# Clamp and low-half subtraction of the weight conversions on GpSimd instead of VectorE, in a pooled attention with two feed-forward products

## The chip, the cores and the metric

The kernel runs on one core of a Trainium2 chip. The metric is the device time of one execution in microseconds (us), the median of several runs. TensorE (PE) multiplies, VectorE (DVE) and ScalarE (ACT) work element by element, GpSimd (POOL) does so too and issues a part of the DMAs, and SyncE (SP) issues the rest.

## The reference

Everything is float32; `moe_w1` and so on are drawn in double precision and are handed over as 64-bit numbers.

```python
# attention: 8 batches, 8 heads, 576 positions, head width 64; k and v are averaged over 8 positions
k_p = k.reshape(B, H, Sp, 8, D).mean(axis=3);  v_p = v.reshape(B, H, Sp, 8, D).mean(axis=3)
attn = softmax(q @ k_p.T / sqrt(D));           x = attn @ v_p          # then 4608 x 512
# first feed-forward
h = ((x @ w1) * (x @ w2)) @ w3                 # 512 -> 1024 -> 1024
x = h @ w_out                                  # 1024 -> 512
# second feed-forward
g = max(x @ w_in, 0) + log1p(exp(-abs(x @ w_in)))    # 512 -> 2048
out = g @ w_out2                               # 2048 -> 512
```

## The kernel before

The kernel first multiplies w3 by w_out (W, 1024 x 512), since nothing stands between the two products: 64 full float32 products `Wp` (L509, in W_mm). Then, block by block of 512 tokens, it computes a = x w1, b = x w2, g = a b and x2 = g W (`ab`, `x2_mm`), while the attention of later tokens runs between these products. Last comes the second feed-forward. Products in the main loops are made of three passes over a high and a low half of each operand (`mm3`, L122 to L124; `split`, L117 and L118).

The weights lie in memory as 64-bit words. w_out, w3, w1 and w2 come in 20 jobs of two tiles of 128 x 512 each: 12 for w_out and w3 (four and eight), 8 for the groups of w1 and w2 (`w12_0` to `w12_7`). A job is: two loads by SP into a ring of four raw places (L130), so that two jobs are in flight; `magnitudes`, the absolute value of the upper word on ACT (L137); then `convert_steps` on DVE: clamp (L146), shift (L148), sign (L151), bits of the lower word (L156). The groups of w1 and w2 are then split: the high half on ACT (L160), the low half by a subtraction on DVE (L163). While one job is between L151 and L156, `ahead` begins the next one: its L137 is issued there. When a job is over, its two raw places are loaded again.

The names in the rows: `wgh_512_...` and `wgl_512_...` are the converted tiles of w_out and w3, `w_0h` and `w_0l` are the two halves of a group of w1 or w2, `area_f` holds raw words and staging, `area_r` the halves that TensorE reads, `ks`, `kT` and `vb` are the averaged keys and values, `sc`, `pr`, `pT` and `pv` the steps of the attention.

Each engine works through its instructions in the order in which the program issues them; the order is written out by hand: a table of slots for the attention (`sched`, run by `att_slot`) and a list of background steps (`bg`) that advances the jobs by one or two steps per slot. GpSimd's own queue before holds the loads of k, v and q (L305, L312, L315) and the copies of the averaged keys (L328).

Of the kernel before, what the change touches and what calls it, by code (L numbers as in the profile page):

```python
# [8 lines left out]
F32 = mybir.dt.float32  # L9
# [3 lines left out]
ALU = mybir.AluOpType  # L13
# [21 lines left out]
HI_MIN = 3.4332275390625e-05 * HI_SCALE  # L35
HI_MAX = 122879.9921875 * HI_SCALE
# [12 lines left out]
def pooled_attention_two_ffn(ctx: ExitStack, tc: tile.TileContext, qT_d, kT_d, v_d, w12_d, w3T_d, wo_d, wi_d, wo2_d, out):  # L49
# [3 lines left out]
    nc = tc.nc  # L53
# [55 lines left out]
    def t2k(name, dt=F32):  # L109
        return t2k_ring[0]([P, 512], dt)  # L110
# [22 lines left out]
    def magnitudes(raws, dsts, name):  # L133
        both = range(len(raws))
        y = dsts or [t2k(f"y_{name}_{i}") for i in both]
        for i in both:
            nc.scalar.activation(y[i], raws[i][:, :, 1].bitcast(F32), AF.Abs, scale=HI_SCALE)  # L137
        return y

    def convert_steps(raws, dsts, y, ahead):  # L140


        both = range(len(raws))
        yi = [t.bitcast(I32) for t in y]
        for i in both:
            nc.vector.tensor_scalar(y[i], y[i], HI_MIN, HI_MAX, op0=ALU.max, op1=ALU.min)  # L146
        for i in both:
            nc.vector.tensor_scalar(yi[i], yi[i], 3, None, op0=ALU.logical_shift_left)  # L148
        yield
        for i in both:  # L150
            nc.vector.scalar_tensor_tensor(yi[i], raws[i][:, :, 1], -0x80000000, yi[i], op0=ALU.bitwise_and, op1=ALU.bitwise_or)  # L151
        yield
        ahead()
        yield
        for i in both:
            nc.vector.scalar_tensor_tensor(yi[i], raws[i][:, :, 0], 29, yi[i], op0=ALU.logical_shift_right, op1=ALU.bitwise_or)  # L156
        yield
        if isinstance(dsts[0], tuple):
            for i in both:
                nc.scalar.activation(dsts[i][0], y[i], AF.Copy)  # L160
            yield
            for i in both:
                nc.vector.tensor_sub(dsts[i][1], y[i], dsts[i][0].bitcast(F32))  # L163

# [12 lines left out]
    def begin_job(k):  # L179
        if len(loaded) > k:  # L180
            name, raws, dst, split_ = loaded[k]
            if name not in begun:
                dsts = None if split_ else dst()
                begun[name] = dsts, magnitudes(raws, dsts, name)

    def next_job():
        load_ahead()
        begin_job(0)
        name, raws, dst, _ = loaded[0]
        dsts, y = begun.pop(name)  # L190
        yield from convert_steps(raws, dsts or dst(), y, lambda: begin_job(1))
        loaded.pop(0)
        converted.add(name)
        load_ahead()
# [699 lines left out]
```

## Time and profile before

| | us |
|---|---|
| median of 3 runs | 1573.36 (1571.50 to 1576.69) |
| span of the profiled execution, first to last instruction | 1572.0 |
| TensorE busy | 1525.3 |
| VectorE busy | 1002.8 |
| ScalarE busy | 769.4 |
| GpSimd busy | 138.6 |

The page gives the span of the profiled execution and no other time for it; the span lies 1.4 us under the median and inside the three runs. Busy shares are means over stages with different limits: the conversions of w_out, w3, w1 and w2 lie in the first 170 us alone. In a timeline row, the first two numbers are start and length in us; "x2" means that two instructions of one form are merged, and what stands in brackets is the engine's idle time ahead of them and what ended it.

### The profile page before, as it was taken

What the parts mean: (1) busy time and instruction counts of PE and PEld (TensorE: products, weight loads), DVE (VectorE), ACT (ScalarE), POOL (GpSimd) and SP (SyncE); (2) the same over time, 40 slices, a digit from 0 to 9 for tenths busy, and PEclk for the clock granted to TensorE, in tenths of its full rate; (3) what the DMA queues carried; (4) which work ended last, traced back from release to release, by engine and by line L of the source; (5) the groups of instructions that cost most, each with busy time, mean ns of one, the idle gap of its engine ahead of it and who ended that gap; (6) DMA issues with size and microseconds to landing.
All of it is one profiled execution on the core that took longest, in us unless ns stands there. A gap on an engine that the chain in (4) does not pass through costs nothing.

```text
span 1572.0 us, 20121 instructions
## 1 busy us (share of the span) xinstructions
PE 1525.3 (97%) x7712; PEld 1283.2 (82%) x7712; DVE 1002.8 (64%) x1514; ACT 769.4 (49%) x1611; POOL 138.6 (9%) x266
## 2 busy tenths in 40 slices
PE   4889999999999999999999999999999999999998
PEld 2448788888888888777889889898988898989897
DVE  7886666556565654222346777677777677678665
ACT  3445444444444443332245566566556556556554
POOL 3200101010100100000110000000000000000000
PEclk9999999999999999999999999999999999999999
DMA  8553244435453532003445336335336335434431
GB/s 287 195 183 122 59 163 153 148 124 182 138 187 129 192 109 72 1 27 134 134 155 179 121 114 202 114 123 193 124 112 204 110 128 167 152 111 130 149 105 40
DMA packets 70943, 215.21 MB, mean 137 GB/s; under 512 B 6848, under 2 KB 26304, under 8 KB 63680
## 3 DMA queue, kind: packets, MB, share of 16 engines
q0 software_dynamic: 24352, 124.79, 24.8%
q1 hardware_dynamic: 46496, 89.14, 16.5%
q8 instruction: 61, 1.00, 0.3%
q14 instruction: 34, 0.28, 0.1%
HBM read 171.97 MB, written 41.94 MB: 136 GB/s over the span
## 4 chain that ended last, share of the span: by engine, by line
PE 91%; DVE 4%; ACT 2%; DMA 2%; issue 1%; POOL 0%; SPq 0%; DVEq 0%; ACTq 0%; POOLq 0%
PE o L766 8%; PE o L765 8%; PE ab L122 8%; PE o L764 8%; PE ab L124 8%; PE ab L123 8%; PE X L123 4%; PE X L124 4%; PE X L122 4%; PE x2p L122 4%; PE x2p L124 4%; PE x2p L123 4%; PE Z L123 3%; PE Z L122 3%; PE Z L124 3%; PE pv L397 2%
## 5 line engine op out<-in xcount | busy, mean ns | idle before, releaser
L117 ACT ACTIVATE area_r<-area_f 128x768 fp32r<-128x768 f32 (+1 forms) x168 | 126.7, 754 | 224.9 <-DVE area_f L563 183.9
L766 PE MATMUL o<-w2h,area_r 128*128 128x512 f32 x576 | 228.2, 396 | 0.3 <-DVE area_r L118 0.3
L765 PE MATMUL o<-w2l,area_r 128*128 128x512 f32 x576 | 227.2, 394 | 0.0
L764 PE MATMUL o<-w2h,area_r 128*128 128x512 f32 x576 | 224.0, 389 | 0.0
L118 DVE TENSOR_TENSOR area_r<-area_f,area_r 128x768 fp32r<-128x768 f32 (+1 forms) x168 | 141.7, 844 | 116.6 <-ACT area_r L117 116.4
L733 ACT ACTIVATE area_f<-area_f 128x768 f32<-128x768 f32 x96 | 81.3, 847 | 124.9 <-DVE area_f L825 123.4
L737 DVE TENSOR_SCALAR area_f<-area_f 128x768 f32<-128x768 f32 x96 | 53.8, 560 | 120.2 <-ACT area_f L734 120.2
L123 PE MATMUL X<-area_r,wf 128*128 128x384 f32 x384 | 129.2, 336 | 0.0
L124 PE MATMUL X<-area_r,wf 128*128 128x384 f32 x384 | 128.9, 336 | 0.0
L122 PE MATMUL X<-area_r,wf 128*128 128x384 f32 x384 | 128.8, 335 | 0.0
L766 PEld LDWEIGHTS o<-w2h,area_r 128*128 128x128 f32 x576 | 108.0, 187 | 23.6 <-DVE area_r L118 0.7
L362 ACT ACTIVATE pr<-sc,mx 128x72 f32<-128x72 f32 x288 | 87.7, 331 | 80.5 <-DVE mx L360 80.5
L563 DVE TENSOR_TENSOR area_f<-area_f,ab 128x512 f32<-128x512 f32 x72 | 49.4, 686 | 115.1 <-PE ab L124 108.4
L764 PEld LDWEIGHTS o<-w2h,area_r 128*128 128x128 f32 x576 | 108.2, 188 | 16.0 <-ACT area_r L117 0.3
L765 PEld LDWEIGHTS o<-w2l,area_r 128*128 128x128 f32 x576 | 108.0, 187 | 15.9
L634 POOL DMA_DIRECT2D wf<-wis x96 | 51.9, 541 | 774.5 <-PE X L124 665.5
L122 PE MATMUL x2p<-area_r 128*128 128x512 f32 x288 | 115.8, 402 | 0.0
L124 PE MATMUL x2p<-area_r 128*128 128x512 f32 x288 | 112.6, 391 | 0.0
L123 PE MATMUL x2p<-area_r 128*128 128x512 f32 x288 | 112.4, 390 | 0.0
L123 PE MATMUL Z<-area_r,wf 128*128 128x384 f32 x288 | 96.8, 336 | 0.0
L743 DVE TENSOR_TENSOR area_f<-area_f 128x768 f32<-128x768 f32 x96 | 92.0, 958 | 6.7 <-ACT area_f L740 0.5
L122 PE MATMUL Z<-area_r,wf 128*128 128x384 f32 x288 | 96.2, 334 | 0.0
(167 smaller groups left out, 3334.5 us busy)
## 6 DMA issues: line engine op xcount, KB each, us to landing
wf<-wis POOLq DMA_DIRECT2D x48, 1024.0 KB, 5.2
wf<-wis POOLq DMA_DIRECT2D x48, 768.0 KB, 4.5
area_f<-in_wo_dram SPq DMA_DIRECT2D x24, 512.0 KB, 4.3
wis<-area_f SPq DMA_DIRECT2D x40, 256.0 KB, 2.6
kv<-in_kT_dram POOLq DMA_DIRECT2D x32, 288.0 KB, 3.9
q<-in_qT_dram POOLq DMA_DIRECT2D x18, 512.0 KB, 5.0
kv<-in_v_dram POOLq DMA_DIRECT2D x32, 288.0 KB, 4.5
x2d<-area_f SPq DMA_DIRECT2D x36, 256.0 KB, 4.0
```

The source lines that it names most:

```text
L117: nc.scalar.activation(hi, src, AF.Copy)
L118: nc.vector.tensor_sub(lo, src, hi.bitcast(F32))
L122: nc.tensor.matmul(ps, whi, xhi, start=first, stop=False, skip_group_check=resumed)
L123: nc.tensor.matmul(ps, whi, xlo, start=False, stop=False, skip_group_check=resumed)
L124: nc.tensor.matmul(ps, wlo, xhi, start=False, stop=last, skip_group_check=resumed)
L362: nc.scalar.activation(pr[:, h, :], sc[h // 4][:, h % 4, :], AF.Exp, bias=mx[:, h:h + 1], scale=SCALE, accum_out=sm[:, h:h + 1])
L733: nc.scalar.activation(e, c, AF.Abs)
L737: nc.vector.tensor_scalar(u, e, 1.0, None, op0=ALU.add)
L743: nc.vector.tensor_add(c, c, u)
L764: nc.tensor.matmul(oacc[s][i], hl[:, 0, ts], wh, start=first, stop=False)
L765: nc.tensor.matmul(oacc[s][i], hl[:, 0, ts], wl, start=False, stop=False)
L766: nc.tensor.matmul(oacc[s][i], hl[:, 1, ts], wh, start=False, stop=last)
```

## The change

The clamp (L146 before) is taken out of `convert_steps` and issued in `magnitudes` on GpSimd, right behind the absolute value of each tile. The subtraction of the low half (L163 before) is issued on GpSimd at the same point of the program. All of the 20 jobs are concerned by the first edit (40 clamps), the 8 jobs of w1 and w2 by the second (16 subtractions). `convert_1024`, the conversion of the second feed-forward's weights, is left as it is.

```diff
 def magnitudes(raws, dsts, name):
     for i in both:
         nc.scalar.activation(y[i], raws[i][:, :, 1].bitcast(F32), AF.Abs, scale=HI_SCALE)
+        nc.gpsimd.tensor_scalar(y[i], y[i], HI_MIN, HI_MAX, op0=ALU.max, op1=ALU.min)
     return y
 def convert_steps(raws, dsts, y, ahead):
...
-    for i in both:
-        nc.vector.tensor_scalar(y[i], y[i], HI_MIN, HI_MAX, op0=ALU.max, op1=ALU.min)
     for i in both:
         nc.vector.tensor_scalar(yi[i], yi[i], 3, None, op0=ALU.logical_shift_left)
...
         for i in both:
-            nc.vector.tensor_sub(dsts[i][1], y[i], dsts[i][0].bitcast(F32))
+            nc.gpsimd.tensor_sub(dsts[i][1], y[i], dsts[i][0].bitcast(F32))
```

From here on the changed kernel has one line less: its L138 is the clamp, its L162 the subtraction, and every other line of the places below has a number that is smaller by one.

GpSimd's queue around the second batch's averaged keys, before (`ks_1` is the second of four pieces; `kv_1_0` is a load of v):

```order
L328 COPY kT_109<-ks_0_449 64x72 x2
L312 DMA kv_0_3_453<-in_kT_dram 128x576
L328 COPY kT_109<-ks_1_472 64x72 x2
L315 DMA kv_1_0_476<-in_v_dram 72x1024
L328 COPY kT_109<-ks_2_513 64x72 x2
L315 DMA kv_1_1_517<-in_v_dram 72x1024
L305 DMA q_537<-in_qT_dram 128x1024
```

The same place in the changed kernel (`wgl_512_320`, `wgh_512_480` and `wgl_512_481` are the jobs wo6, w3_6 and w3_7):

```order
L138 TENSOR_SCALAR wgl_512_320<-wgl_512_320 128x512 x2
L327 COPY kT_109<-ks_0_449 64x72 x2
L311 DMA kv_0_3_453<-in_kT_dram 128x576
L327 COPY kT_109<-ks_1_472 64x72 x2
L314 DMA kv_1_0_476<-in_v_dram 72x1024
L138 TENSOR_SCALAR wgh_512_480<-wgh_512_480 128x512 x2
L327 COPY kT_109<-ks_2_513 64x72 x2
L314 DMA kv_1_1_517<-in_v_dram 72x1024
L138 TENSOR_SCALAR wgl_512_481<-wgl_512_481 128x512 x2
L304 DMA q_539<-in_qT_dram 128x1024
```

The clamps of a job now stand in GpSimd's queue behind copies and loads of the attention, and loads of k, v and q behind clamps.

VectorE's queue over the same stretch, before:

```order
L146 TENSOR_SCALAR wgl_512_320<-wgl_512_320 128x512 x2
L148 TENSOR_SCALAR wgl_512_320<-wgl_512_320 128x512 x2
L325 TENSOR_REDUCE ks_0_449<-kv_0_0_194 128x72
L151 SCALAR_TENSOR_TENSOR wgl_512_320<-area_f,wgl_512_320 128x512 x2
L325 TENSOR_REDUCE ks_1_472<-kv_0_1_211 128x72
L156 SCALAR_TENSOR_TENSOR wgl_512_320<-area_f,wgl_512_320 128x512 x2
L146 TENSOR_SCALAR wgh_512_480<-wgh_512_480 128x512 x2
L148 TENSOR_SCALAR wgh_512_480<-wgh_512_480 128x512 x2
L151 SCALAR_TENSOR_TENSOR wgh_512_480<-area_f,wgh_512_480 128x512 x2
L118 TENSOR_TENSOR area_r<-pv_486,area_r 128x4x128
```

And in the changed kernel:

```order
L147 TENSOR_SCALAR wgl_512_320<-wgl_512_320 128x512 x2
L324 TENSOR_REDUCE ks_0_449<-kv_0_0_196 128x72
L150 SCALAR_TENSOR_TENSOR wgl_512_320<-area_f,wgl_512_320 128x512 x2
L324 TENSOR_REDUCE ks_1_472<-kv_0_1_213 128x72
L155 SCALAR_TENSOR_TENSOR wgl_512_320<-area_f,wgl_512_320 128x512 x2
L147 TENSOR_SCALAR wgh_512_480<-wgh_512_480 128x512 x2
L150 SCALAR_TENSOR_TENSOR wgh_512_480<-area_f,wgh_512_480 128x512 x2
L118 TENSOR_TENSOR area_r<-pv_488,area_r 128x4x128
```

Two instructions per job are gone from VectorE, and the shift (L147) is now the first of a job there; it waits for GpSimd, where L146 waited for ScalarE. ScalarE's, TensorE's and SyncE's own orders stay as they were.

## Rows read from the trace of the kernel before

**Rows 1.** The page's first part: busy time, share of the span, instructions.

```profile
PE 1525.3 (97%) x7712; PEld 1283.2 (82%) x7712; DVE 1002.8 (64%) x1514; ACT 769.4 (49%) x1611; POOL 138.6 (9%) x266
```

**Rows 2.** Stretches: busy us (instructions) by engine, TensorE's granted clock, DMA share, GB/s.

```profile
0.00:110.00 110.00, 79.07 (x257) 39.88 (x257) 88.88 (x175) 45.65 (x122) 23.93 (x47) 0.91 0.71 235
110.00:175.00 65.00, 62.59 (x354) 50.74 (x353) 46.43 (x92) 31.60 (x98) 6.51 (x12) 1.00 0.31 100
```

**Rows 3.** Chain that ended last, in order of time: start, us, what.

```profile
12.14 6.45 DMA kv<-in_v_dram
...
20.96 0.67 DVE wgl L146 x2
...
34.43 4.44 DMA area_f<-in_w3T_dram
38.89 0.69 ACT wgl L137
39.60 0.43 DVE wgl L146
...
40.61 1.29 DVE wgl L151 x2
...
58.06 0.67 DVE wgl L146 x2
...
65.53 0.67 DVE wgl L146 x2
...
70.59 0.67 DVE wgh L146 x2
...
77.31 8.96 DMA area_f<-in_w_dram
...
87.48 1.98 PE pv L397 x16
89.45 20.77 PE Wp L509 x44
```

**Rows 4.** TensorE's waits from 0 to 110 us: us in total, times, longest.

```profile
PE pv L397 <- ACT pT L380: 4.0, 1, 4.0
```

**Rows 5.** The two moved lines by themselves: ns shortest/median/longest, first and last start.

```profile
L146 DVE TENSOR_SCALAR wgh<-wgh x12: 417/420/427, 5.0 to 70.8; 128x512 f32<-128x512 f32 x12
L163 DVE TENSOR_TENSOR w_0l<-area_f,w_0h x2: 679/680/681, 93.0 to 93.6; 128x512 fp32r<-128x512 f32 x2
```

**Rows 6.** GpSimd's timeline at the start, and its copies (L328) by themselves.

```profile
0.25 0.10 POOL L882 MEMSET const-float32-0.0<- 128x1 f32 x1 [0.25 <-issue]
...
0.74 0.20 POOL masks.py:197 MEMSET ident<- 128x128 f32 x1 [0.29 <-POOLq L882]
1.03 0.29 POOL masks.py:199 TENSOR_SCALAR_AFFINE_SELECT ident<-ident 128x128 f32<-128x128 f32 x1
...
L328 POOL COPY kT<-ks x64: 236/243/3591, 10.6 to 602.4; 64x72 f32<-64x72 f32 x64
```

**Rows 7.** Timelines of GpSimd, then of VectorE, from 69 to 74 us.

```profile
69.65 3.87 POOL L328 COPY kT<-ks 64x72 f32<-64x72 f32 x2
73.47 0.53 POOL L315 DMA_DIRECT2D kv<-in_v_dram  x1
...
69.31 1.28 DVE L156 SCALAR_TENSOR_TENSOR wgl<-area_f,wgl 128x512 int32<-128x512 int32 x2
70.51 0.76 DVE L146 TENSOR_SCALAR wgh<-wgh 128x512 f32<-128x512 f32 x2
71.18 0.76 DVE L148 TENSOR_SCALAR wgh<-wgh 128x512 int32<-128x512 int32 x2
71.86 1.28 DVE L151 SCALAR_TENSOR_TENSOR wgh<-area_f,wgh 128x512 int32<-128x512 int32 x2
73.06 0.69 DVE L118 TENSOR_TENSOR area_r<-pv,area_r 128x512 fp32r<-128x512 f32 x1
```

**Rows 8.** TensorE's waits from 100 to 200 us: us in total, times, longest.

```profile
PE pTp L379 <- DVE pr L370: 3.1, 3, 1.7
```

**Rows 9.** Timelines of ScalarE and TensorE: last group's high half, first use of its low half.

```profile
167.24 1.14 ACT L160 ACTIVATE w_7h<-area_f 128x512 fp32r<-128x512 f32 x2
...
173.41 0.39 PE L124 MATMUL ab<-area_r,w_7l 128*128 128x512 f32 x1
```

## The prediction

> **What bounds the kernel now.** I read the busy shares first: TensorE is busy for 97% of the span [rows 1]. Only stretches in which it waits can be moved by an edit on other engines, so the next view is the one by stretches. Up to 110 us TensorE works for 79 us, with the other 31 us lost at the start and between products, while VectorE is busy for 89 of the 110 and the DMA engines for 71%; from 110 to 175 us TensorE waits for 2.4 us in all [rows 2]. All 20 jobs that the change touches lie in these two stretches; what follows is the same work in the same order, and it starts earlier or later by what they gain or lose.
>
> So the third view is the chain of work that ended last, within the first 110 us [rows 3]. It runs through a load of v at 12 us, several conversions of w_out and w3 on VectorE, a load of raw words at 34 us, an absolute value and a clamp at 39 us, the second load of raw words at 77 us, and from 89.45 us through 44 products in a row. Two points of it matter. The load at 77.31 us can start only when VectorE has ended job w3_6, since it takes that job's raw places; it takes 8.96 us. And TensorE's wait of 4.0 us ahead of the pv products at 87.48 us is a wait for ScalarE's copy [rows 4], which stands in ScalarE's queue behind the absolute value that wants this load. Whatever makes w3_6 end later on VectorE therefore shifts 87.48 us, and everything behind it, by as much.
>
> **What is taken off VectorE.** A clamp lasts 0.42 us by itself and a low half 0.68 us [rows 5]; in a row two clamps take 0.67 us of VectorE's time [rows 3], and two low halves overlap in the same way, so I count 1.2 us for them, an estimate. That is 20 times 0.67 and 8 times 1.2, some 23 us of VectorE's 1003. It is no gain by itself: only the clamps on the chain count.
>
> **What one costs on GpSimd.** No such clamp or subtraction runs there before, so I bound it by GpSimd's own rows [rows 6]. A memset of one column takes 0.10 us and one of 128 columns 0.20 us, which is 0.0008 us a column over a fixed 0.10; the affine select reads and writes 128 columns in 0.29 us, 0.0015 a column; a copy of 72 columns takes 0.243 us, 0.0020 a column over the same 0.10. For 512 columns this gives 0.51, 0.86 and 1.12 us; the copy taken as a plain ratio of columns gives 1.73. I take c = 0.86 us for a clamp, since the affine select is the row that is most like it (all partitions, one input, one output, arithmetic in between), with 0.51 and 1.73 as the ends. A subtraction reads a second input: I add a memset's 0.0008 a column and take s = 1.3 us, between 0.86 and 3.46 (twice 1.73). The Trainium skill (GPSIMD Engine Reference, Engine selection) says that one-input work on GpSimd runs at about line rate and two-input work at about half of VectorE's speed. An estimate from that page, 512 columns at its 1.2 GHz, would be 0.43 us for the clamp; by it the sum below would be about 0.
>
> **Can they run beside VectorE?** This is the point on which the sum rests. Two copies on GpSimd that take 0.24 us each stood there for 3.87 us from 69.65 us. VectorE went through L156, L146, L148 and L151 in that time without a gap, and the copies ended when it came to L118, which reads PSUM and one operand of SBUF [rows 7]. So GpSimd doesn't get at SBUF while VectorE runs conversion steps back to back: neither between two of them nor beside them. A clamp on GpSimd runs when VectorE waits, reduces or reads PSUM; otherwise it runs when VectorE has come to the shift that needs it, and then both clamps of the job are paid in full.
>
> **Term by term, up to 110 us.**
> - T1, clamps that are ready in time. At three places of the chain (20.96, 27.03 and 58.06 us; the first and the last in [rows 3]) VectorE ahead of the clamp reduces, waits or reads PSUM, so the clamps are over and 0.67 us goes away: 3 times -0.67 = -2.0 us.
> - T2, the job clamped at 65.53 us (wo6). Its absolute values are written while VectorE normalizes and runs L156. Both clamps then follow one another: 2c - 0.67 = +1.05 (ends +0.35 and +2.79). The same happens at 34.3 us, off the chain: the load at 34.43 us covers it [rows 3].
> - T3, the job at 39.60 us, whose words arrive last of all. From the end of the absolute value (39.58) to the sign step (40.61) it is 1.03 us now [rows 3]; a clamp of c and a shift of 0.42 in its place make c - 0.61 = +0.25 (ends -0.10 and +1.12).
> - T4, the job clamped at 70.59 us (w3_6). Its clamps stand in GpSimd's queue behind the two copies of `ks_1` and the load of `kv_1_0`. The copies can't start before VectorE has ended L156 of the job ahead, as they couldn't before [rows 7]. VectorE's shift thus waits for two copies (0.49), the issue of a DMA (0.53) and two clamps, against 0.67 now: 0.49 + 0.53 + 2c - 0.67 = +2.07 (ends +1.37 and +3.81). This is the largest term, a wait in the place of the work removed; behind that shift on VectorE stand L118 and the maxima, and TensorE's scores wait for L118.
> - T5, the load of v at 12.14 us on the chain [rows 3]. It is now issued behind both clamps of the second job; 0 to 2c later, and I take half, c = +0.86.
> - T6, w3_7's second clamp, which may hold SBUF when VectorE wants it for w3_6's last step: 0 to c, and I take a third, +0.3.
>
> Sum: -2.0 + 1.05 + 0.25 + 2.07 + 0.86 + 0.3 = +2.5 us.
>
> **From 110 to 175 us.** TensorE waits for VectorE's normalization three times, 3.1 us in all [rows 8]. What is ahead of each is the product of a and b, ScalarE's copy and exp; no clamp or low half is in that chain, so none of it is won. A clamp of the next job can hold SBUF when the normalization is due: 0 to c, taken at half, +0.4. The low halves have time. The tightest is the last group's: its high half ends at 168.38 us and TensorE wants the low one at 173.41 [rows 9], 5.0 us for two subtractions of 2s = 2.6 us.
>
> Together +2.9 us, or 6.83c - 2.93 as a function of c. Against the profiled execution, 1572.0 + 2.9 = 1574.9 us; its span is 1.4 us under the median, so on the median's scale 1573.4 + 2.9 = **1576 us**. A measurement of this kernel can tell about 0.3% (4.7 us) from no change, so this forecast is "no change that can be told".
>
> **The rivals.**
> - Slower: GpSimd's clamp is dear. One mechanism, T2, T4 and T5 with a larger c. By the function above the shift reaches 4.7 us at c = 1.12 us, which is what the copy's rate gives; at c = 1.73 it is +8.9 us, 1582 us. For it: the copies are the only rows of GpSimd that read computed data and write it elsewhere, and rows 7 show how long it can be kept off SBUF. Against it: most of a copy's 0.24 us may be fixed cost.
> - Faster: GpSimd does run beside VectorE, and the copies of rows 7 waited for something else. Then the five pairs of clamps on the chain go at 0.67 us each, -3.35, and the load of 77.31 us, which begins earlier, may find the DMA engines freer; -3 to -6 us, 1567 to 1570 us. Against it stands every instant of [rows 7].
> - Fair turns: GpSimd waits for the instruction that runs on VectorE, not for the whole row of them. T4's copies and DMA would then be over when L156 ends and T4 falls by 0.49 + 0.53 = 1.0: +1.9 us, 1575 us. The Trainium skill (SBUF — State Buffer, SBUF: two separate sides) describes the pair of ports shared by VectorE and GpSimd as a lock that whoever starts first holds for one whole instruction, which would allow such turns; the 3.87 us in rows 7 span eight instructions and speak against it.
> - The edit does nothing: the load of 8.96 us at 77.31 us shrinks by what it starts later, and TensorE's wait of 4.0 us swallows the rest: 1573 us. I count it with the forecast, since it has no sign.
>
> **How the numbers follow.** Forecast (c between 0.51 and 1.12, or the case without effect): 0.55, no change that can be told. Fair turns: 0.10, the same. Dear clamp: 0.25, slower by over 0.3%. Side by side: 0.10, half of it within 0.3% and half faster. So faster 0.05, same 0.70, slower 0.25. The low end is the forecast with c = 0.51 and T5, T6 and the normalization at nothing: -2.0 + 0.35 - 0.10 + 1.37 = -0.4, that is 1573, less 2 us for the spread of the runs and the edge of the side-by-side case: 1571. The high end reaches to the dear clamp's 1582. What lies outside is the faster half of one rival and subtractions dearer still.
>
> **What would show it.** In the profile of the changed kernel: a clamp of 0.8 to 0.9 us where VectorE is idle, and stretched ones where it isn't (c); VectorE waiting for GpSimd at the shift of wo6, w3_3 and w3_6, with some 2 us at w3_6 (T2 to T4); no wait at the shifts of w3_1, wo2 and w3_5 (T1); the load of w12_0 starting near 80 us instead of 77.31 and TensorE's 44 products ending near 112.7 instead of 110.2; the stretch from 175 us on as long as now. The forecast is wrong if VectorE's conversion steps get longer while GpSimd works, if GpSimd's clamps start between two of them, or if TensorE comes to wait for a low half.

## The result, and the profile after

The changed kernel takes 1593.0 us in the median (1592.28 to 1594.9, 4 runs) against 1574.12 us before (1571.5 to 1576.69, 4 runs): a ratio of 1.012, with a 95% interval from 1.0104 to 1.0136. That is +18.9 us (16.4 to 21.4), where the prediction had +2.9 and a range that ended at 1582. The profiled execution has a span of 1591.6 us, 19.6 more than before.

The page's busy shares come first; they answer to [rows 1].

```profile
PE 1527.5 (96%) x7712; PEld 1284.1 (81%) x7712; DVE 997.8 (63%) x1458; ACT 770.5 (48%) x1611; POOL 242.9 (15%) x322
```

Fifty-six instructions have gone to GpSimd, and its busy time rose by 104 us. VectorE lost the same 56 but only 5.0 us of busy time. The prediction had counted some 23 us taken off VectorE. TensorE works 2.2 us longer, so nearly all of the loss is waiting.

The view by stretches (columns as in [rows 2]) says where; the third stretch is one within the second.

```profile
0.00:110.00 110.00, 68.01 (x233) 34.12 (x234) 74.04 (x126) 38.15 (x109) 80.79 (x76) 0.89 0.65 213
110.00:175.00 65.00, 58.42 (x282) 42.86 (x281) 45.06 (x65) 30.96 (x79) 46.05 (x28) 0.95 0.33 107
...
125.00:130.00 5.00, 5.00 (x13) 3.84 (x13) 5.00 (x9) 2.33 (x5) 2.04 (x2) 0.50 0.30 120
```

TensorE works 68.0 instead of 79.1 us up to 110 us, and 58.4 instead of 62.6 from there to 175. The loss is where the prediction looked for it.

The chain of work that ended last, in order of time, answers to [rows 3]. Before, the chain's only steps on GpSimd were copies of keys and the issue of a load, up to 12.1 us.

```profile
42.59 3.97 POOL wgl L138 x2
...
57.05 4.71 DMA area_f<-in_w3T_dram
62.53 4.58 POOL wgl L138 x2
...
71.90 4.26 POOL wgl L138 x2
...
81.10 3.81 POOL wgh L138 x2
...
89.03 4.27 POOL wgl L138 x2
...
109.19 4.40 POOL w_0l L162 x2
113.59 3.78 POOL area_f L138 x2
...
118.80 2.76 DVE area_f L150 x2
122.26 1.17 ACT w_2h L159 x2
```

A pair of clamps (L138) takes 3.8 to 4.6 us on the chain, where [rows 3] had 0.67 us for a pair on VectorE. The next view has groups of the two moved lines by themselves (ns shortest/median/longest, first and last start), as [rows 5] had them on VectorE.

```profile
L138 POOL TENSOR_SCALAR wgh<-wgh x12: 1904/1912/2368, 5.0 to 83.0; 128x512 f32<-128x512 f32 x12
L138 POOL TENSOR_SCALAR wgl<-wgl x12: 1904/2164/3251, 18.3 to 90.9; 128x512 f32<-128x512 f32 x12
L162 POOL TENSOR_TENSOR w_0l<-area_f,w_0h x2: 1261/2215/3169, 109.2 to 112.3; 128x512 fp32r<-128x512 f32 x2
L162 POOL TENSOR_TENSOR w_6l<-area_f,w_6h x2: 1287/1292/1297, 172.6 to 173.9; 128x512 fp32r<-128x512 f32 x2
```

The clamp takes 1.91 us where it is undisturbed, above the upper end that the prediction gave it (1.73), and up to 3.25 us. The subtraction takes the 1.3 us that it was taken at, but one of w_0l takes 3.17. Undisturbed, the instruction with one input is dearer than the one with two.

What VectorE waits for, until the end of w3_6's last step (us in total, times, longest): first the whole list after, to 91.6 us, then the two rows of the kernel before that answer to its first two, to 77.3 us.

```profile
DVE wgh L147 <- POOL wgh L138: 16.6, 8, 7.0
DVE wgl L147 <- POOL wgl L138: 5.0, 6, 1.1
DVE sm L367 <- ACT pr L361: 3.9, 3, 1.6
DVE vb L335 <- DMA kv<-in_v_dram: 2.9, 2, 2.3
DVE ks L324 <- POOL kT L327: 1.5, 1, 1.5
DVE mx L358 <- PE sc L347: 1.5, 2, 1.1
...
DVE wgh L146 <- ACT wgh L137: 7.0, 4, 5.0
DVE wgl L146 <- ACT wgl L137: 1.1, 2, 0.8
```

And the stretch up to that step's end by engine (columns as in [rows 2]), before and after, with e15 (below), in which nobody clamps, as the third.

```profile
0.00:77.24 77.24, 50.69 (x178) 26.63 (x179) 61.09 (x125) 29.84 (x85) 21.73 (x43) 0.91 0.72 241
...
0.00:91.52 91.52, 50.64 (x176) 26.07 (x177) 59.76 (x103) 31.10 (x94) 65.61 (x64) 0.88 0.63 206
...
0.00:75.61 75.61, 48.30 (x176) 24.93 (x177) 54.01 (x103) 28.65 (x81) 18.91 (x43) 0.94 0.75 247
```

These two views are the account of the first stage. VectorE reaches the end of w3_6 at 91.52 instead of 77.24 us, 14.3 us late. It stands idle for 31.8 instead of 16.2 us in these stretches, 15.6 more: 21.6 instead of 8.1 us ahead of a job's first steps, +13.5, and 2.1 elsewhere, mostly for keys, values and the softmax. Its busy time fell by 1.3 us only. The 22 clamps of this stretch had made up 7.1 us of it, since without them VectorE is busy for 54.0 us in e15: what it kept became 5.8 us longer. 15.6 - 1.3 = 14.3.

The lengthening shows where the two engines work side by side, here in the timelines of GpSimd and VectorE (start, length in us) from 71 to 79 us.

```profile
71.90 4.25 POOL L138 TENSOR_SCALAR wgl<-wgl 128x512 f32<-128x512 f32 x2 [4.80 <-ACT wgl L137]
77.33 1.29 POOL L327 COPY kT<-ks 64x72 f32<-64x72 f32 x2 [1.19 <-DVE ks L324]
...
72.41 1.70 DVE L155 SCALAR_TENSOR_TENSOR wgl<-area_f,wgl 128x512 int32<-128x512 int32 x2
...
77.19 1.33 DVE L150 SCALAR_TENSOR_TENSOR wgl<-area_f,wgl 128x512 int32<-128x512 int32 x2
```

The pair at 72.41 lies wholly inside the first of the two clamps and takes 1.70 instead of 1.28 us [rows 7]; that clamp takes 2.37 us and the second, beside no such pair, 1.91. The copies behave as in [rows 7]: two of them, of 0.24 us each when undisturbed, end at 78.62, when VectorE's pair of 77.19 ends at 78.52.

Not every clamp gets in like this. The longest one (3.25 us, of the two at 26.57) came while VectorE ran two pairs in a row, and these kept their length:

```profile
26.57 5.13 POOL L138 TENSOR_SCALAR wgl<-wgl 128x512 f32<-128x512 f32 x2
...
25.55 1.28 DVE L150 SCALAR_TENSOR_TENSOR wgl<-area_f,wgl 128x512 int32<-128x512 int32 x2
26.75 1.28 DVE L155 SCALAR_TENSOR_TENSOR wgl<-area_f,wgl 128x512 int32<-128x512 int32 x2
```

So did the subtraction of 3.17 us at 109.19, beside two pairs of 1.28 us each. What decides between the two cases is not shown.

The second loss follows from 110 us. Timelines of TensorE, then of ScalarE:

```profile
118.35 1.88 PE L508 MATMUL Wp<-wgl,wgl 128*128 128x512 f32 x4
124.70 0.79 PE L122 MATMUL ab<-area_r,w_0h 128*128 128x512 f32 x1 [4.47 <-DVE area_r L118]
...
122.26 1.17 ACT L159 ACTIVATE w_2h<-area_f 128x512 fp32r<-128x512 f32 x2 [5.68 <-DVE area_f L155]
```

The 44 products end near 120.2 instead of 110.2 us: 10.0 of the 14.3 us have come through. Then TensorE waits 4.47 us for the low half of Wp, whose high half stands on ScalarE behind w_2h, and so behind VectorE's steps of w12_2, whose clamps stand on GpSimd behind the subtractions of w_0l (the rows at 109.19 to 122.26 of the chain). Two of these rows are longer than their work: the subtractions take 4.40 us for two, and VectorE's pair at 118.80 takes 2.76 us, beside the next subtraction and a clamp. The first product of `ab` is 15.0 us late (109.66 before). After that wait the granted clock is 0.50 from 125 to 130 us, the lower of its levels (1.2 and 2.4 GHz), and products come 0.43 us apart instead of 0.23. The scores at 115.64 before come at 133.24, 17.6 late. The lateness grows to 19.4 us by 175 us, in waits and not at a lower clock; from there on the two executions run alike.

### The profile page after: what moved, and what is told of

Same layout as the page of the kernel before. It is cut to its first block, busy times and chain, and to the rows that moved or that the text cites. A ratio compares the mean times of both kernels' runs of the same rounds, so it can differ in the third digit from the quotient of the medians.

```text
span 1591.6 us, 20123 instructions
## 1 busy us (share of the span) xinstructions
PE 1527.5 (96%) x7712; PEld 1284.1 (81%) x7712; DVE 997.8 (63%) x1458; ACT 770.5 (48%) x1611; POOL 242.9 (15%) x322
## 4 chain that ended last, share of the span: by engine, by line
PE 86%; DVE 5%; POOL 3%; ACT 3%; DMA 2%; issue 1%; SPq 0%; DVEq 0%; ACTq 0%; POOLq 0%
PE o L765 8%; PE o L764 8%; PE o L763 8%; PE ab L122 8%; PE ab L124 8%; PE ab L123 7%; PE X L123 4%; PE X L124 4%; PE X L122 4%; PE x2p L122 4%; PE x2p L124 4%; PE x2p L123 4%; PE Z L123 3%; PE Z L124 3%; PE Z L122 3%; PE pv L396 2%
## 5 line engine op out<-in xcount | busy, mean ns | idle before, releaser
L123 PE MATMUL Z<-area_r,wf 128*128 128x384 f32 x288 | 96.8, 336 | 0.0
L124 PE MATMUL Z<-area_r,wf 128*128 128x384 f32 x288 | 96.2, 334 | 0.0
L122 PE MATMUL Z<-area_r,wf 128*128 128x384 f32 x288 | 96.1, 334 | 0.0
```

The costliest lines, as they stand in the source:

```text
L122: nc.tensor.matmul(ps, whi, xhi, start=first, stop=False, skip_group_check=resumed)
L123: nc.tensor.matmul(ps, whi, xlo, start=False, stop=False, skip_group_check=resumed)
L124: nc.tensor.matmul(ps, wlo, xhi, start=False, stop=last, skip_group_check=resumed)
```

## The experiments

Every kernel below is the kernel before with the edit shown, but for e6 and e13, which are edits of the changed kernel, and for those that name another run as theirs. Line numbers differ by a few between kernels.

**e1, e2: one edit at a time.** The clamps alone on GpSimd, and the subtractions alone.

```diff
# e1
+            nc.gpsimd.tensor_scalar(y[i], y[i], HI_MIN, HI_MAX, op0=ALU.max, op1=ALU.min)
...
-        for i in both:
-            nc.vector.tensor_scalar(y[i], y[i], HI_MIN, HI_MAX, op0=ALU.max, op1=ALU.min)
# e2
-                nc.vector.tensor_sub(dsts[i][1], y[i], dsts[i][0].bitcast(F32))
+                nc.gpsimd.tensor_sub(dsts[i][1], y[i], dsts[i][0].bitcast(F32))
```

> Only the clamps are on GpSimd; the low halves stay on VectorE. Theory A (VectorE waits for clamps that take 1.9 us instead of 0.42): job w3_6 ends about 14 us later on VectorE as in the changed kernel, TensorE's wait ahead of the pv products swallows 4 us of it, and the clamp of w12_2 no longer stands behind the subtraction of w_0l, so the wait of 4.5 us ahead of the first product of a and b shrinks: 1584 to 1589 us. Rival B (the low halves cost most of it): 1574 to 1578 us.

> Only the low halves are on GpSimd; the clamps stay on VectorE. Theory A: the subtractions have time everywhere and VectorE loses 10 us of work that was not on the chain: 1573 to 1577 us. Rival B (the subtractions, 1.27 us each, hold up VectorE's conversion steps and the split of W behind them): 1580 us or more.

Measured: e1 1588.53 us, ratio 1.009 (1.0075 to 1.0105); e2 1574.6 us, ratio 1.0005 (0.9996 to 1.0014). The clamps alone make three quarters of the loss. The subtractions alone cost nothing that can be told; the last quarter needs both.

**e3: the clamps of the first twelve jobs only.**

```diff
+            if dsts:
+                nc.gpsimd.tensor_scalar(y[i], y[i], HI_MIN, HI_MAX, op0=ALU.max, op1=ALU.min)
...
+            if isinstance(dsts[0], tuple):
+                nc.vector.tensor_scalar(y[i], y[i], HI_MIN, HI_MAX, op0=ALU.max, op1=ALU.min)
```

> The clamps of the 12 jobs of w_out and w3 alone are on GpSimd; those of w1 and w2 and all low halves stay on VectorE. Theory A: job w3_6 still ends 14 us later, the 44 products end some 10 us later, and from there on all is as before: 1583 to 1586 us. Rival C (the loss is made behind the products, by the split of W that waits for the conversion of w12_2): 1578 us or less.

Measured: 1586.36 us, ratio 1.0078 (1.0061 to 1.0095). The jobs of w_out and w3 carry nearly all that clamps alone cost.

**e4: clamps that nobody waits for.** VectorE keeps its clamps, and GpSimd does 24 more, on a tile that nobody reads, where the first twelve jobs have theirs.

```diff
+    scratch = mem(GBUF + 14, [P, 512], F32R)
...
+            if dsts:
+                nc.gpsimd.tensor_scalar(scratch, scratch.bitcast(F32), HI_MIN, HI_MAX, op0=ALU.max, op1=ALU.min)
```

> The kernel before, with 24 clamps more on GpSimd, at the places where the changed kernel has those of the 12 jobs of w_out and w3, on a scratch tile that nobody reads. VectorE clamps as before and waits for none of them. Theory A (the wait for the clamp's result is what costs): the loads of k and v in GpSimd's queue come 2 to 4 us later and little else: 1574 to 1579 us. Rival D (GpSimd's work beside VectorE slows VectorE down, whoever waits): as much as with the clamps of the 12 jobs in use, 1583 us or more.

Measured: 1590.18 us, ratio 1.0101 (1.0086 to 1.0116). The theory that only the wait for a clamp's result costs is gone: here there is none. But the run mixes two things. VectorE's own steps are longer, and it waits for values that GpSimd loads late, behind clamps in its queue (VectorE's waits up to 120 us):

```profile
DVE vb L340 <- DMA kv<-in_v_dram: 11.0, 4, 6.6
```

In the changed kernel this wait is 2.9 us. TensorE waits 3.98 us ahead of the first product of `ab` here too, with the clamps and subtractions of w1 and w2 on VectorE. The next runs take the two apart.

**e5: what the forms cost.** Two sets of nine GpSimd instructions on idle tiles at the program's start; part of the edit:

```diff
+            nc.gpsimd.tensor_copy(b, a)
+            nc.gpsimd.tensor_scalar(b, a, HI_MIN, None, op0=ALU.max)
+            nc.gpsimd.tensor_scalar(b, a, HI_MIN, HI_MAX, op0=ALU.max, op1=ALU.min)
...
+            nc.gpsimd.tensor_scalar(b, a, 1.0, 0.0, op0=ALU.mult, op1=ALU.add)
```

> The kernel before with eighteen extra GpSimd instructions on idle 512-column tiles ahead of its first loads (nobody reads them; read from the second nine): a copy, a maximum alone, maximum and minimum, the same on 256 columns, a product alone, a product and a sum, maximum and minimum in place, a subtraction, a product of two tiles. Theory 1, the clamp is dear because it has two operations in one instruction: the one-operation forms take 0.9 to 1.3 us, maximum-and-minimum and product-and-sum both 1.8 to 2.0, in place or not. Theory 2, it is dear because of maximum and minimum: product-and-sum stays at 1.0 to 1.3 and a maximum alone takes 1.3 to 1.9. Theory 3, it is dear because it is written in place: out of place 1.0 to 1.3, in place 1.9. In all three the subtraction of two tiles takes 1.25 to 1.3. The whole time, 10 to 30 us above the kernel before, since the key and value loads are issued behind these instructions, is not the question.

Timeline of GpSimd, the second set, in the order of the expectation (the product of two tiles, 1.26 us, is left out):

```profile
16.03 0.61 POOL L477 COPY area_f<-area_f 128x512 f32<-128x512 f32 x1
16.72 1.49 POOL L478 TENSOR_SCALAR area_f<-area_f 128x512 f32<-128x512 f32 x1
18.29 1.92 POOL L479 TENSOR_SCALAR area_f<-area_f 128x512 f32<-128x512 f32 x1
20.29 1.06 POOL L480 TENSOR_SCALAR area_f<-area_f 128x256 f32<-128x256 f32 x1
21.44 1.50 POOL L481 TENSOR_SCALAR area_f<-area_f 128x512 f32<-128x512 f32 x1
23.02 0.62 POOL L482 TENSOR_SCALAR area_f<-area_f 128x512 f32<-128x512 f32 x1
23.72 1.92 POOL L483 TENSOR_SCALAR area_f<-area_f 128x512 f32<-128x512 f32 x1
25.72 1.26 POOL L484 TENSOR_TENSOR area_f<-area_f 128x512 f32<-128x512 f32 x1
```

The kernel took 1593.95 us in its one run. None of the three theories fits whole. In place or not makes no difference (1.92 both). Two operations are not dear as such: product and sum take 0.62 us, as little as a copy, while a product alone or a maximum alone takes 1.50. Maximum and minimum take 1.92, and 1.06 on half the columns. The price depends on which operations stand in the instruction, and no row of the kernel before showed a maximum on GpSimd.

**e6: the changed kernel with a shorter clamp.**

```diff
-            nc.gpsimd.tensor_scalar(y[i], y[i], HI_MIN, HI_MAX, op0=ALU.max, op1=ALU.min)
+            nc.gpsimd.tensor_scalar(y[i], y[i], HI_MIN, None, op0=ALU.max)
```

> The changed kernel with the clamp cut to its first operation, the maximum (the upper bound of the magnitudes is left out). If the size of the clamp is the term that was wrong and a maximum alone takes 0.9 to 1.3 us instead of 1.9, the time falls from 1593 to 1578 to 1584. If GpSimd's mere presence beside VectorE, or its queue, is what costs, the time stays at 1588 or above, though the clamp is shorter. If the maximum alone takes 1.9 us too, the run says nothing: 1592 to 1594.

Measured: 1585.24 us, ratio 1.0061 (1.0038 to 1.0084), with 1.48 us for the undisturbed clamp. A cut of 0.4 us in the clamp gives back half the loss, +9.6 instead of +18.9. The medians lie between the two expectations, but on the side of the clamp's size. TensorE's 4.47 us wait for the low half of Wp is not there.

**e7, e8: the same six jobs, without the queue.** In e7 twelve clamps that nobody waits for, in e8 the real ones, at jobs with no copy, key or value load near in GpSimd's queue.

```diff
+    MID = ("w3_2", "w3_3", "wo4", "w3_4", "w3_5", "wo6")
# e7
+            if name in MID:
+                nc.gpsimd.tensor_scalar(scratch, scratch.bitcast(F32), HI_MIN, HI_MAX, op0=ALU.max, op1=ALU.min)
# e8
+            if name in MID:
+                nc.gpsimd.tensor_scalar(y[i], y[i], HI_MIN, HI_MAX, op0=ALU.max, op1=ALU.min)
...
+            if name not in MID:
+                nc.vector.tensor_scalar(y[i], y[i], HI_MIN, HI_MAX, op0=ALU.max, op1=ALU.min)
```

> The kernel before with twelve clamps more, on a tile that nobody reads, on GpSimd behind the magnitudes of six jobs (w3_2, w3_3, wo4, w3_4, w3_5, wo6) near which no copy of key sums and no key or value load stands in GpSimd's queue. Theory A, only the wait for a clamp's result costs: 1573 to 1575. Theory Q, only copies and loads that stand behind clamps in GpSimd's queue cost: 1573 to 1575. Theory D, VectorE's own instructions last longer while GpSimd works: about 0.3 us for each of the twelve, VectorE some 3 to 4 us late by 70 us, the time 1576 to 1578, and the two-input instructions of these jobs 0.2 us or more longer in the mean.

> The clamps of the same six jobs really on GpSimd, all other clamps and all low halves on VectorE. Theory A, with 1.9 us for the clamp in place of the 0.86 of the prediction: wo6 waits 3.1, w3_3 1.3, four jobs give back 0.67 each, so +1 to +3: 1574.5 to 1577. Theory D: these and the 3 to 4 us of VectorE's own longer instructions: 1578 to 1581. Theory Q: as A.

Measured: e7 1575.57 us, ratio 1.0005 (0.9992 to 1.0019); e8 1580.71 us, ratio 1.0033 (1.0021 to 1.0045). In e7's trace VectorE begins the last step of w3_6 at 79.48 instead of 75.91 us, 3.57 late, 0.30 us for each of the twelve clamps. Its two-input line by itself (ns shortest/median/longest):

```profile
L162 DVE SCALAR_TENSOR_TENSOR wgl<-area_f,wgl x12: 677/685/1106, 23.0 to 87.5; 128x512 int32<-128x512 int32 x12
```

Most instructions keep their 0.68 us and those that meet a clamp take 1.10: so VectorE is slowed as theory D said, but the time hardly moved, which it did not say. TensorE's wait for pT fell from the 3.96 us of [rows 4] to 1.94. In e8 VectorE waits 9.0 us for these clamps and is 7.56 us late at w3_6. It is spared six pairs of clamps, 0.67 us each in a row [rows 3], 4.0 us in all, yet it is busy for 61.6 us to the end of that step, where it was 61.1 before: what it kept is some 4.5 us longer. The wait for the result and the slower steps are both real, and the time lies where theory D put it.

**e9, e10: does that wait of TensorE swallow the delay?** e9 is the kernel before without the early magnitudes of w12_0; e10 is e9 with the clamps of e7.

```diff
-        if len(loaded) > k:
+        if len(loaded) > k and not (k == 1 and loaded[k][0] == "w12_0"):
```

> The kernel before, with both edits out, and one other thing changed: the magnitudes of w12_0 are not begun ahead, so ScalarE's copy of pT no longer stands behind the 8.96 us load of w12_0, for which TensorE waits 3.96 us at 87.48. Theory: the wait goes and nothing else is late next, so the time falls by 3 to 4 us, to 1570 to 1572. Rival: VectorE or the load itself is late next (the first product of stage A at 109.66 waits for w12_0 or for the low half of Wp instead), 1573 to 1575.

> The last kernel with the twelve clamps on a tile that nobody reads, at the same six jobs as in e7_extra_mid. There VectorE was 3.57 us late at w3_6 (79.48 against 75.91) and the time rose by 0.6 only. If TensorE's wait of 3.96 us for pT swallowed that delay, it costs its full size here, where the wait is gone: 3 to 3.6 us above e9_late_abs. If the delay meets slack elsewhere, this kernel takes the time of e9_late_abs within 1 us.

Measured: e9 1575.91 us, ratio 1.0007 (0.9997 to 1.0017); e10 1577.96 us, ratio 1.0024 (1.0013 to 1.0036). TensorE in e9:

```profile
85.10 1.09 PE L397 MATMUL pv<-pT,vb 72*64 72x128 f32 x16
...
94.58 1.53 PE L509 MATMUL Wp<-wgh,wgh 128*128 128x512 f32 x2 [2.17 <-DVE area_r L118]
```

The wait ahead of pv is gone, as expected, but nothing is gained: 2.17 us of waiting came in its place at 94.58, and the first product of `ab` starts at 108.85, 0.8 us earlier than before. The expected gain of 3 to 4 us did not come. e10 is 2.1 us above e9 by the medians, 2.7 by the ratios, against 3 to 3.6 expected and 0.6 to 0.8 between e7 and the kernel before. In the traces VectorE is 4.2 us later than in e9 at w3_6 (81.72 against 77.53) and the first product of `ab` 4.5 (113.34 against 108.85). There the delay comes through whole, where in e7 3.57 us came out as 1.09, as if slack in TensorE's wait for pT had taken up a part in e7. This is not settled: the times lean the same way, but their intervals leave it open, and the trace of e10 is of a run 2.3 us above its median, that of e9 of one 2.5 us below. The slack is no fixed amount either: from the issue of w12_0's first load to the second absolute value it takes 9.6 us before, 8.0 in e7, 10.4 in e6 and 5.4 in the changed kernel.

**e11: one job.** Only the clamps of w3_6 on GpSimd (the edit of e8 with one name in the list).

```diff
+    MID = ("w3_6",)
```

> Only the two clamps of w3_6 on GpSimd, everything else as before. By term T4 of the prediction with 1.9 us in place of 0.86 (0.49 + 0.53 + 3.8 - 0.67) VectorE is 4.1 us late at the last step of w3_6 (80.0 instead of 75.91), of which TensorE's wait for pT can swallow up to 3.5: 1574.5 to 1577. If the wait behind the two copies and the key load is not what made this job 4.5 us longer in the changed kernel, VectorE is less than 2.5 us late there, and the time is 1573 to 1574.5.

Measured: 1577.12 us, ratio 1.0015 (1.0006 to 1.0025). Timelines of GpSimd and then of VectorE:

```profile
68.50 1.52 POOL L333 COPY kT<-ks 64x72 f32<-64x72 f32 x2 [23.24 <-DVE ks L330]
69.97 0.55 POOL L317 DMA_DIRECT2D kv<-in_kT_dram  x1
70.56 1.33 POOL L333 COPY kT<-ks 64x72 f32<-64x72 f32 x2
71.83 0.54 POOL L320 DMA_DIRECT2D kv<-in_v_dram  x1
72.44 3.82 POOL L141 TENSOR_SCALAR wgh<-wgh 128x512 f32<-128x512 f32 x2
...
81.18 1.33 DVE L161 SCALAR_TENSOR_TENSOR wgh<-area_f,wgh 128x512 int32<-128x512 int32 x2
```

The clamps stand behind copies and loads as term T4 said, and VectorE needs 10.96 us from wo6's last step to w3_6's (70.22 to 81.18) instead of 6.60 (69.31 to 75.91): +4.4, where T4's formula with 1.9 us gives 4.15. In the changed kernel the same stretch is 4.5 us longer.

**e12: clamps of w1 and w2 back on VectorE.** e3 with the low halves on GpSimd.

```diff
-                nc.vector.tensor_sub(dsts[i][1], y[i], dsts[i][0].bitcast(F32))
+                nc.gpsimd.tensor_sub(dsts[i][1], y[i], dsts[i][0].bitcast(F32))
```

> The clamps of the twelve jobs of w_out and w3 and all low halves on GpSimd; the clamps of w1 and w2 on VectorE. If the 4.5 us between the changed kernel and clamps alone came from the clamps of w12_2, which stood behind the subtractions of w_0l in GpSimd's queue, this kernel is as e3_first12: 1585.5 to 1588. If low halves on GpSimd cost 4 us as soon as VectorE runs late for whatever reason, it is at 1590 to 1592.

Measured: 1587.6 us, ratio 1.0089 (1.007 to 1.0109), the same as e3 within the intervals. TensorE's wait ahead of `ab` isn't there either. Subtractions on GpSimd cost in the changed kernel because clamps of w1 and w2 stand among them; that it is those of w12_2 is read from the chain.

**e13, e14: a cheap instruction in the clamp's place.** e13 is the changed kernel, e14 the kernel e1, each with the 0.62 us form. **e15** leaves the clamps out.

```diff
# e13, e14
-            nc.gpsimd.tensor_scalar(y[i], y[i], HI_MIN, HI_MAX, op0=ALU.max, op1=ALU.min)
+            nc.gpsimd.tensor_scalar(y[i], y[i], 1.0, 0.0, op0=ALU.mult, op1=ALU.add)
# e15
-        for i in both:
-            nc.vector.tensor_scalar(y[i], y[i], HI_MIN, HI_MAX, op0=ALU.max, op1=ALU.min)
```

> The changed kernel with the clamp on GpSimd replaced by a product with 1 and a sum with 0 (the bounds of the magnitudes are left out), which took 0.62 us by itself in e5_forms. The formula of the prediction, 6.83 c - 2.93, gives +1.3 with c = 0.62: 1575 to 1577.5. If that holds, the size of the clamp was the only term that was wrong. If the steps failed beside it (VectorE's own instructions slowed by GpSimd, the split of Wp behind w12_2), the time stays 4 us or more above the kernel before: 1578.5 to 1583.

> The same cheap instruction in place of the clamps, with all low halves on VectorE (the bounds of the magnitudes are left out). If the low halves cost nothing where the clamps are cheap, as e2_low_only says, this is within 1.5 us of e13_cheap_both. If a subtraction on GpSimd costs by standing ahead of a clamp, however short that is, this one is 2 us or more below it.

> The kernel before with the clamps of these conversions left out on both engines: what it is worth at most to take them from VectorE. VectorE has 9.0 us of them before the last step of w3_6. If that stretch is VectorE's, 5 to 9 us are gained: 1566 to 1570. If loads and the chain of the attention steps set its length as much, at most 3: 1571.5 to 1574.

Measured: e13 1578.53 us, ratio 1.0024 (1.0014 to 1.0034); e14 1576.33 us, ratio 1.0013 (1.0003 to 1.0022); e15 1570.3 us, ratio 0.9974 (0.9964 to 0.9984). What taking the clamps off VectorE could have won at best is thus 4.1 us, between the two expectations of e15. (The 9.0 us named there are the clamps' own lengths; VectorE's busy time falls by 7.1 us.) Even a GpSimd instruction of 0.62 us loses the 4.1 us and 2 us more (e14). e13's median lies at the lower edge of its second expectation, by which more than the clamp's size was wrong. VectorE's timeline in e13 shows how:

```profile
65.37 2.11 DVE L155 SCALAR_TENSOR_TENSOR wgl<-area_f,wgl 128x512 int32<-128x512 int32 x2
```

The pair takes 2.11 instead of 1.28 us beside GpSimd. Between e13 and e14 lie 1.7 us by the ratios, which decides for neither expectation.

## Why the prediction was wrong, step by step

The forecast was "no change that can be told" and the kernel is 1.2% slower. The "dear clamp" rival named the right direction, and put its end at +8.9 us.

**The term that was mis-sized is c.** It was taken as 0.86 us with 0.51 and 1.73 as the ends, and measured 1.91. The bounds came from rows of other operations on fewer columns, as if columns were what counts. e5 shows that they are not: at the same 512 columns GpSimd takes 0.61 to 1.92 us depending on the operation. The upper end was no bound at all. The estimate from the Trainium skill (GPSIMD Engine Reference, Engine selection), 0.43 us for one-input work at line rate, lies somewhat below the copy (0.61) and the product with a sum (0.62); for the clamp the measurement is four times as long and decides. s was right for a subtraction that is not held up (1.3 against 1.26 to 1.29).

**What c explains, and what it doesn't.** The formula 6.83 c - 2.93 at three prices of the instruction by itself:

| kernel | c, us | formula | measured, us |
|---|---|---|---|
| e13 | 0.62 | +1.3 | +3.8 (2.2 to 5.4) |
| e6 | 1.50 | +7.3 | +9.6 (6.0 to 13.2) |
| changed kernel | 1.91 | +10.1 | +18.9 (16.4 to 21.4) |

At the two lower prices it falls short by 2.5 and 2.3 us, at the price of the changed kernel by 8.8. With the right c the forecast would have been 1583.5 us and "slower"; about half of the loss would still be missing. That it comes close at the lower prices does not prove its terms: in the changed kernel they are off in both directions, as follows.

**"GpSimd doesn't get at SBUF while VectorE runs conversion steps" was wrong** for these instructions, and with it the assumption that what stays on VectorE keeps its length. Most clamps that meet such steps start and run beside them, and both last longer: 5.8 of the 7.1 us that the edit took off VectorE up to w3_6 came back in this way. The prediction read its rule from two copies [rows 7]. The copies still behave so, and so do the clamp of 3.25 us and the subtraction of 3.17 us; it was wrong of clamps like the one at 71.90 us. It had named longer conversion steps as a sign of failure. Here the Trainium skill (SBUF — State Buffer, SBUF: two separate sides) has a lock that is held for a whole instruction; by it the pair of 72.41 us could not have run inside a clamp that had started first, and the row at 71.90 disagrees.

**T1** counted three clamps as given back, and one was. At w3_1 the shifts do not wait; at wo2 and w3_5 VectorE waits 1.05 and 0.87 us. Up to 91.6 us it waits for GpSimd ahead of 14 shifts, in 8 of 11 jobs. **T2 to T4** are the right mechanism with too small a c. With 1.9 us they would be 3.1, 1.3 and 4.15 us. VectorE's lateness grows by 1.6 us over wo6 (8.17 to 9.79), half of what T2 would be, by 1.35 over w3_3 (5.38 to 6.73), and by 4.5 over w3_6, which e11 shows alone with 4.4. The first job adds 1.96 us and w3_4 2.7, which no term had. **T5**: the load of v comes at 16.10 instead of 12.14 us, 3.96 late and not 0.86, behind the four clamps of the first two jobs; VectorE waits 2.9 us for values in the stretch. **T6** is part of the 5.8 us.

**"Whatever makes w3_6 end later on VectorE therefore shifts 87.48 us, and everything behind it, by as much" was wrong.** The 14.3 us came out as 10.0 at the end of the 44 products; in e7 3.57 came out as 1.09 at the first product of `ab`. The rival in which the load shrinks and TensorE's wait swallows the rest had described this; e9 and e10 do not settle it. The table has the profiled executions, VectorE's last step of w3_6 and the first product of `ab`.

| kernel | VectorE late, us | `ab` late, us | span longer, us |
|---|---|---|---|
| e7 | 3.57 | 1.09 | 1.3 |
| e11 | 5.27 | 3.17 | 4.0 |
| e8 | 7.56 | 5.81 | 6.9 |
| e3 | 13.15 | 12.49 | 12.6 |
| changed kernel | 14.33 | 15.04 | 19.6 |

**From 110 to 175 us** the prediction had +0.4 us and "the low halves have time". It asked whether TensorE waits for a low half, and it doesn't. It did not ask what stands behind a subtraction on GpSimd: the clamps of w12_2, and through them ScalarE's w_2h and the split of Wp. That is the 4.47 us wait at 124.70, with the lower granted clock after it. From this cause it appears only with the dear clamp and the subtractions of that stage together: e1 (subtractions on VectorE) has 1.41 us, e6 (1.48 us for the clamp) and e12 (clamps of that stage on VectorE) none. The 3.98 us of e4 at the same place have another cause; its chain there begins with values that are loaded late. From the first product of `ab` to the scores it takes 8.54 us at the lower clock, 2.6 more than before (5.98). No run changes the clock alone; e4, where the granted clock falls to 0.50 in its wait too, takes 7.94 us, and e1, e3, e6 and e12, whose granted clock stays at 1.00, take 5.71 to 5.98.

## What to carry to other kernels

Price an operation on another engine by that operation: here rows of other operations bounded the clamp's price not even from above. Work moved beside a busy engine takes a part of what it gave, since both slow each other: compare the gain of leaving the work out (4.1 us for the clamps here) with what the move must then pay in waits and slower steps. And follow each moved instruction's queue to what stands behind it, since two edits that are harmless or mild alone can meet there.

## What the runs showed of the hardware

- GpSimd on 128 x 512 float32: copy 0.61 us, product and sum 0.62, a maximum or a product alone 1.50, maximum and minimum 1.92, subtraction of two tiles 1.26.
- Most clamps on GpSimd and two-input steps on VectorE that meet run side by side. VectorE's instruction takes 1.10 instead of 0.68 us and the clamp 2.1 to 2.4 instead of 1.9. A one-input shift beside a clamp takes up to 0.83 instead of 0.42. One clamp (3.25 us) and one subtraction (3.17) were held up instead while VectorE kept its pace. Copies of 72 columns end with VectorE's pair (1.29 us for two that take 0.24 each).
- The two loads of w12_0's raw words, at the same place of the program, were in 5.4 to 10.4 us after the first one's issue, from kernel to kernel; that spread is larger than most effects that were looked for here.
